# A third layer as 7 block products for 8, with its weights streamed for each token block

## The chip, the cores and the metric

The kernel runs on one NeuronCore of one Trainium2 chip. The metric is the device time of one execution, in microseconds (us). The kernel before takes 916.54 us (median of 3 runs, 916.5 to 916.63).

## The reference

Attention over 4 batches, 8 heads, 576 positions of 64 (window of 32 positions in half of the heads, the same dilated by 4 in the others) gives `x` of 2304 tokens by 512. Two feed-forward networks follow it, all in float32:

```python
x    = attention(q, k, v)                       # [2304, 512]
gate = 1.0 / (1.0 + np.exp(-(x @ w_gate)))      # 512 -> 1536
y    = (gate * (x @ w_val)) @ w_out             # 1536 -> 512
h    = y @ w_in                                 # 512 -> 2048, the "third layer"
g    = np.maximum(h, 0.0) + alpha * np.minimum(h, 0.0)
out  = g @ w_out2                               # 2048 -> 512
```

The weights come as float64 and are decoded on the chip.

## The kernel before

Every float32 product is made of three passes of float16 matmuls: each operand is scaled by a power of two and split into a high half `hi` and the rest `lo`, and hi·hi, hi·lo and lo·hi are added in PSUM (`passes`, L476). The high half is a ScalarE (ACT) activation, the low half a VectorE (DVE) instruction that reads the source and the high half (`split_act`, L168 to L170); weights use `split_weight` (L198), two ACT passes and a subtraction on POOL (L166).

The work falls into four stages. The first follows a list written out by hand (`FIRST`): attention of batch 0 and its gate and value products, until about 180 us. Then a loop over batches 1 to 3 does twelve steps of gate and value products (`gv_mm`, L588, 288 columns) and four of the second layer (`o1_mm`, L630, 72 matmuls each). Attention of the next batch is put between them by two tables (`before`, `after`): softmax on DVE and POOL, a 32x32 transpose (L404), its halves (`p_hi` on ACT L408, `p_lo` on POOL L166) and the product with the values on TensorE (PE) (L435). Between all of this `prepare` runs `steps`, the decoding and splitting of the last two layers' weights, as a budget of columns allows: of `w_in` the split is done by `in2_split` and stored to `wi_dram`; of `w_out2` seven block sums are built (`out2_sums`, DVE, L767 to L770), split (L777 ACT, L782 DVE) and stored to `w2_dram`. During batch 3 four tiles `w_i` (1 MB each, all of `w_in` in halves) are loaded and stay.

The last stage begins at 556.9 us and is what the change rewrites. The 2304 tokens go in five blocks, four of 512 and one of 256. For each block the third layer has 16 column tiles (`in2_mm`, L836 to L849: 12 matmuls each, 512 tokens wide, into one of four PSUM banks). Each tile is evicted by `in2_evac`: ACT takes relu(-h) (L881), DVE adds alpha times it to h (the slope, L882). Tiles k and k + 8 are a pair: `g_sums` makes four block sums of it on POOL (L893 to L896, 256 wide), and seven parts are split, highs on ACT (`g_high`, L905), lows on DVE (`g_low`, L908). The fourth layer already runs as 7 block products for 8: `out2_mm` (L925 to L946) is an item (product i, pair k) of 6 matmuls 256 wide, 56 items a block; its weights come through a ring of four 1 MB slots (`w2_fetch`, L916 to L923, 35 fetches). The items of a block are put between the tiles of the next block, 3 or 4 behind each. `out2_done` (L948 to L967) evicts a product and writes the result. The next block's activations come by `y_load` (L826) and `y_split` (L828). PE runs in program order, and so does each other engine; a tile's bank comes free when its slope on DVE is done.

## Time and profile before

| what | before |
|---|---|
| median of 3 runs | 916.54 us (916.5 to 916.63) |
| the profiled execution | 915.95 us, span 914.2 us |
| mean granted TensorE clock | 0.966 |
| busy: PE, DVE, ACT, POOL | 868.0, 620.9, 447.9, 285.8 us |
| last stage, 556.9 to 910.4 us | 353.5 us: PE busy 352.56, DVE 233.17, ACT 169.86, POOL 122.17 |
| bytes moved by DMA | 131.08 MB |

The page gives the busy time of each engine over the span of one profiled execution; the span is 1.75 us shorter than that execution's own time. The granted clock is TensorE's as a share of 2.4 GHz. A timeline row has the start, the length, the engine, the line and the operation, and in brackets the idle time before it with the work that ended it. Matmuls overlap, so the price of one in a stream is the distance between the starts of two rows divided by the count, not a row's length.

### The profile page before, as it was taken

How to read it: one execution, taken by the hardware profiler on the slowest of the kernel's cores; microseconds unless marked ns; L12 is line 12 of the kernel's file. 1: busy time of each engine (PE TensorE's matmuls, PEld its weight loads, DVE VectorE, ACT ScalarE, POOL GpSimd, SP SyncE). 2: the span in 40 equal slices, each digit the busy share in tenths (PEclk: the TensorE clock that was granted, in tenths of full speed). 3: DMA queues.
4: the chain of work that ended last, by engine and by line, in shares of the span. 5: the costliest groups of instructions: out<-in, count | busy, mean ns of one | idle time of the engine just before them, and what ended most of it. 6: DMA issues, size and time to landing. Idle time of an engine off the chain costs nothing.

```text
span 914.2 us, 18416 instructions
## 1 busy us (share of the span) xinstructions
PE 868.0 (95%) x7636; PEld 645.8 (71%) x7636; DVE 620.9 (68%) x1004; ACT 447.9 (49%) x821; POOL 285.8 (31%) x311
## 2 busy tenths in 40 slices
PE   7878888899999799999999999999999999999998
PEld 5566666687777577877888775456666666667887
DVE  5999999724767455667775662996666676667452
ACT  4776565445344466434434554674444444444441
...
GB/s 322 270 229 119 158 108 161 39 59 178 49 50 174 136 145 217 25 1 165 240 162 196 210 258 273 79 46 105 57 164 137 104 116 127 104 105 123 144 161 219
DMA packets 114179, 131.08 MB, mean 143 GB/s; under 512 B 33200, under 2 KB 100912, under 8 KB 109104
## 3 DMA queue, kind: packets, MB, share of 16 engines
...
## 4 chain that ended last, share of the span: by engine, by line
PE 74%; DVE 16%; ACT 3%; DMA 3%; issue 2%; POOL 1%; SPq 0%; DVEq 0%; POOLq 0%; ACTq 0%
PE banks L588 22%; PE banks L846 20%; PE banks L939 18%; PE banks L630 10%; DVE plain L181 4%; PE banks L435 3%; DVE plain L185 3%; DVE plain L177 2%; DVE gf L606 1%; DMA words<-w_gate 1%; PE banks L321 1%; DVE rs L379 1%; DMA second<-kt 1%; DVE vh L280 1%; POOL s L166 1%
## 5 line engine op out<-in xcount | busy, mean ns | idle before, releaser
L588 PE MATMUL banks<-xh,w_gv 128*128 128x288 f16 x2304 | 297.7, 291 | 0.1
L588 PEld LDWEIGHTS <-w_gv 128*128 128x128 f16 x2304 | 226.4, 99 | 61.0
L846 PE MATMUL banks<-yh,w_i 128*128 128x512 f16 (+1 forms) x960 | 197.6, 358 | 0.9 <-DVE yh L170 0.9
L846 PEld LDWEIGHTS <-w_i 128*128 128x128 f16 x960 | 93.8, 98 | 83.6 <-issue 1.5
L630 PE MATMUL banks<-gt,w_o 128*128 128x288 f16 x1152 | 151.0, 295 | 0.1
L630 PEld LDWEIGHTS <-w_o 128*128 128x128 f16 x1152 | 114.6, 101 | 32.5 <-DVE w_o L170 0.6
L881 ACT ACTIVATE neg<-banks 128x512 f32<-128x512 f32 (+1 forms) x80 | 44.0, 550 | 140.7 <-PE banks L846 140.7
L939 PE MATMUL banks<-w,g_g 128*128 128x256 f16 x600 | 76.8, 273 | 0.0
L606 DVE SCALAR_TENSOR_TENSOR gf<-banks,sg 128x576 f32<-128x576 f32 x48 | 36.1, 752 | 57.7 <-PE banks L588 53.0
L939 PE MATMUL banks<-w,g_o 128*128 128x256 f16 x570 | 73.7, 273 | 0.0
L192 ACT ACTIVATE junk<-plain 128x1024 bf16<-128x1024 f32 (+1 forms) x36 | 36.3, 1007 | 75.9 <-DVE plain L196 42.2
L882 DVE SCALAR_TENSOR_TENSOR f<-neg,sc,banks 128x512 f32<-128x512 f32 (+1 forms) x40 | 27.7, 692 | 60.6 <-ACT neg L881 60.6
L939 PEld LDWEIGHTS <-g_g 128*128 128x128 f16 x600 | 58.7, 98 | 10.9
L181 DVE SCALAR_TENSOR_TENSOR plain<-words,plain 128x512 uint32<-128x512 uint32 x68 | 64.1, 963 | 1.2
L939 PEld LDWEIGHTS <-g_o 128*128 128x128 f16 x570 | 55.8, 98 | 10.5
L882 DVE SCALAR_TENSOR_TENSOR temps_a<-neg,sc,banks 128x512 f32<-128x512 f32 (+1 forms) x40 | 27.7, 693 | 52.2 <-ACT neg L881 52.2
L166 POOL TENSOR_TENSOR gt<-gf,gt 128x576 f16<-128x576 f32 x24 | 37.4, 1558 | 79.8 <-ACT gt L613 79.8
L185 DVE SCALAR_TENSOR_TENSOR plain<-words,plain 128x512 uint32<-128x512 uint32 x68 | 58.9, 886 | 1.2
L893 POOL TENSOR_TENSOR temps_a<-f,f 128x256 f32<-128x256 f32 (+1 forms) x20 | 16.4, 818 | 133.2 <-DVE f L882 133.2
L601 ACT ACTIVATE sg<-banks,sc 128x576 f32<-128x576 f32 x48 | 35.2, 734 | 39.3 <-PE banks L588 34.7
L613 ACT ACTIVATE gt<-gf 128x576 f16<-128x576 f32 x48 | 32.4, 676 | 42.0 <-DVE gf L606 42.0
L162 POOL TENSOR_SCALAR sc<-sc 128x1 f32<-128x1 f32 (+1 forms) x35 | 11.9, 340 | 129.2 <-DVE sc L158 119.6
...
## 6 DMA issues: line engine op xcount, KB each, us to landing
w<-w_dram SPq DMA_DIRECT2D x35, 1024.0 KB, 5.0
...
```

The costliest lines, as they stand in the source:

```text
L166: engine.tensor_tensor(out=lo, in0=src, in1=hi, op=ALU.subtract)
L181: nc.vector.scalar_tensor_tensor(out=d, in0=hi, scalar=0xC0000000, in1=d, op0=ALU.bitwise_and, op1=ALU.bitwise_or)
L185: nc.vector.scalar_tensor_tensor(out=d, in0=lo, scalar=29, in1=d, op0=ALU.logical_shift_right, op1=ALU.bitwise_or)
L192: nc.scalar.activation(junk[:, :src.shape[1]], src, AF.Square, accum_out=dst)
L588: nc.tensor.matmul(ps[:, h, :], lhsT=a, rhs=x_[:, H2 * h:H2 * h + H2], start=(kk == 0 and i == 0), stop=(kk == KD - 1 and i == 2),)
L601: nc.scalar.activation(halves(sg), ps, AF.Sigmoid, scale=sgx[b][:, m:m + 1])
L606: nc.vector.scalar_tensor_tensor(out=halves(gf), in0=ps, scalar=2.0 ** -15, in1=halves(sg), op0=ALU.mult, op1=ALU.mult)
L630: nc.tensor.matmul(ps[:, h, :], lhsT=a, rhs=x_[:, H2 * h:H2 * h + H2], start=(m == 0 and z == 0), stop=(m == M1 - 1 and z == 2),)
L846: nc.tensor.matmul(ps[:, :n], lhsT=a, rhs=x_, start=(kk == 0 and i == 0), stop=(kk == KD - 1 and i == 2))
L881: nc.scalar.activation(t[:, :n], ps[:, :n], AF.Relu, scale=-1.0)
L882: nc.vector.scalar_tensor_tensor(out=gf[:, :n], in0=t[:, :n], scalar=slope[:, m:m + 1], in1=ps[:, :n], op0=ALU.mult, op1=ALU.add)
L939: nc.tensor.matmul(ps[:, H4 * t:H4 * t + H4], lhsT=a, rhs=x_, start=(first and k == 0 and t == 0 and z == 0), stop=(k == U - 1 and z == 2) ...
```

## The change

The third layer becomes 7 block products for 8 too. In four blocks of 512 tokens, tokens, inputs and columns are halved into quarters, and seven products of sums of quarters (P1 to P7, the Winograd form of Strassen's scheme) give the four quarters of h. A block has four units (`unit`), each of 7 products of 12 matmuls 256 wide; behind each product come two items of the fourth layer (`spare`). Products that belong together are added in PSUM; where they aren't, ACT copies a bank to SBUF (`copy`) and DVE adds the next product to the copy (`plus`). A relu is 512 wide still, a slope two instructions 256 wide, a split of a part 512 wide for what were two of 256. The block of 256 tokens comes first, as plain products (`unit_short`, two tiles at once: an x product on three banks in turn, a y product always on the same bank).

The weights of the third layer are now seven blocks for four and don't all stay: `wi_dram` holds 8 pieces of 896 KB, two of which make a unit's, and for every block all 8 are fetched, into four slots (block 0: also the four slots of the fourth layer's ring, which is not needed yet). A unit gives its two slots back at its end, and only then are the next two pieces and the fourth layer's weights fetched, in SP's queue. Building them takes 4 DVE additions for each u (`in2_sums`), the highs go to ACT and the lows to DVE, so that POOL's subtraction of 1024 columns is gone; in return `out2_sums` moves from DVE to POOL, as do sums of quarters of y (`y_sums`). `prepare` has a larger budget.

```diff
     H4 = DM // 2
     TB = 512
     scale = 0.125
-    blocks = [(t, min(TB, NT - t)) for t in range(0, NT, TB)]
+    T0 = NT % TB
+    blocks = [(0, T0)] + [(t, TB) for t in range(T0, NT, TB)]
     NJ = len(blocks)
+    DIRECT = 0
...
+    wi_dram = dp.tile([U, P, 2, 7, 2 * P], F16, name="wi_dram")
...
+    def in2_sums(u):
+        a21, a11, a12, a22 = (plain["i", u][:, 2 * i:2 * i + 2] for i in range(4))
+        t = plain["is", u] = yp.tile([P, 4, 2, P], F32, tag="y", name="is")
+        add = nc.vector.tensor_tensor
+        add(out=t[:, 0], in0=a21, in1=a22, op=ALU.add)
+        add(out=t[:, 1], in0=t[:, 0], in1=a11, op=ALU.subtract)
+        add(out=t[:, 2], in0=a11, in1=a21, op=ALU.subtract)
+        add(out=t[:, 3], in0=a12, in1=t[:, 1], op=ALU.subtract)
...
-    def in2_split(u):
-        w = plain["ih", u] = yp.tile([P, 2, 4, 256], F16, tag="y", name="halves")
-        t = flat(plain.pop(("i", u))).rearrange("p (k f) -> p k f", k=4)
-        split_weight(w[:, 0], w[:, 1], t, s_i[:, 2 * u:2 * u + 1])
...
+    def in2_high(u):
+        plain["ih", u] = [yp.tile([P, 2, n, 2 * P], F16, tag="y", name="halves") for n in (3, 4)]
+        for w, src in in2_parts(u):
+            nc.scalar.activation(w[:, 0].rearrange("p n f -> p (n f)"), src, AF.Copy, scale=s_i[:, u:u + 1])
+
+    def in2_low(u, i):
+        w, src = in2_parts(u)[i]
+        nc.vector.scalar_tensor_tensor(
+            out=w[:, 1].rearrange("p n f -> p (n f)"), in0=src, scalar=s_i[:, u:u + 1],
+            in1=w[:, 0].rearrange("p n f -> p (n f)"), op0=ALU.mult, op1=ALU.subtract,
+        )
...
+    def in2_fetch(u, ring=ring_i):
+        if not ring_i and not w_i:
+            ring_i.extend(w2p.tile([P, 2, 7, 2 * P], F16, name=f"w_i{n}", tag=f"w_i{n}") for n in range(4))
+        t = ring.popleft()
+        homes.append((ring, t))
+        if ring is not ring_i:
+            t = t.rearrange("p z u f -> p (z u f)")[:, :14 * 2 * P].rearrange("p (z i f) -> p z i f", z=2, i=7)
+        w_i.append(t)
+        nc.sync.dma_start(out=t, in_=wi_dram[u])
+
+    def in2_release():
+        for _ in range(2):
+            w_i.popleft()
+            ring, t = homes.popleft()
+            ring.append(t)
...
-        add = nc.vector.tensor_tensor
+        add = nc.gpsimd.tensor_tensor
...
+    def y_sums(j, d):
...
+        s = y[j, d, "sums"] = yp.tile([P, 4, TB // 2], F32, tag="y", name="ys")
+        add = nc.gpsimd.tensor_tensor
+        if j == DIRECT:
+            add(out=s[:, 0, :n], in0=t[:, 1, :n], in1=t[:, 0, :n], op=ALU.subtract)
+            return
+        b11, b12, b21, b22 = (t[:, i, n // 2 * h:n // 2 * h + n // 2] for i in range(2) for h in range(2))
+        add(out=s[:, 0], in0=b12, in1=b11, op=ALU.subtract)
+        add(out=s[:, 1], in0=b22, in1=s[:, 0], op=ALU.subtract)
+        add(out=s[:, 2], in0=b22, in1=b12, op=ALU.subtract)
+        add(out=s[:, 3], in0=b21, in1=s[:, 1], op=ALU.subtract)
...
+    PART_A = {1: 0, 2: 1, 4: 2, 5: 3, 6: 4, 7: 5, 3: 6}
+    PART_B = {1: 0, 2: 1, 3: 2, 5: 3, 6: 4, 7: 5, 4: 6}
+    in2_banks = {}
+    in2_order = []
+
+    def in2_bank(x_):
+
+        turn["h"] = (turn["h"] + (x_ != "y")) % 3
+        in2_banks[x_] = banks[:, in2_order[3 if x_ == "y" else turn["h"]], :]
...
+        total_ = len(terms) * 6
+        for v in range(2):
+            o = ps[:, n * v:n * v + n]
+            q = 0
+            for a, b in terms:
+                for d in range(2):
+                    c = slice(P * d, P * d + P)
+                    for h, l in passes((w[v][:, 0, a, c], w[v][:, 1, a, c]), (yh[j][0][:, d, b, :n], yh[j][1][:, d, b, :n])):
+                        q += 1
+                        nc.tensor.matmul(
+                            o, lhsT=h, rhs=l, start=(new and v == 0 and q == 1), stop=(q == total_),
+                            skip_group_check=True,
+                        )
         return ps
 
...
+    def unit_short(j, k, spare):
+
+        w = [w_i[0], w_i[1]]
+        u = 2 * k
+        ps = in2_mm(j, "x", [(0, 0), (1, 1)], True, w)
+        spare(3)
+        sums_high()
+        sums_low(4)
+        prelu(j, u, "a11 0", ps)
+        spare(4)
+        ps = in2_mm(j, "y", [(3, 0), (2, 2)], True, w)
+        spare(4)
+        prelu(j, U + u, "a12", ps)
+        a11, a21, a12, a22 = quarters(j, k)
+        parts = [g_high(j, i, k, x_) for i, x_ in ((1, a11), (4, a22), (2, a12))]
+        for t in parts:
+            g_low(*t)
+        spare(3)
+        s = g_sums(j, k)
+        late_.extend((j, i, k, x_) for i, x_ in s)
+
+
+
+    left = [[] for _ in range(7)]
+    begun_units = set()
+
+    def unit_begin(j, k, w):
+        begun_units.add((j, k))
+        copy("c1", in2_mm(j, "x1", [(PART_A[1], PART_B[1])], True, w))
+
+    def unit(j, k, spare, following=None):
+        w = [w_i[0], w_i[1]]
+        u = 2 * k
+        a11, a21, a12, a22 = quarters(j, k)
+        f11 = temps[f"a11 {k % 2}"]
+        t, h = {}, {}
+        if (j, k) not in begun_units:
+            unit_begin(j, k, w)
+        in2_banks["x"] = in2_banks.pop("x1")
+
+        def mm(i, x_, new=False):
+            return in2_mm(j, x_, [(PART_A[i], PART_B[i])], new, w)
+
+        def rest(i):
+            for f in left[i]:
+                f()
+            left[i] = []
+
+        def later(i, f):
+            left[i].append(f)
+
+        def high(i, x_):
+            h[i] = g_high(j, i, k, x_)
+
+        ps = mm(2, "y", True)
+        rest(0)
+        nc.vector.tensor_tensor(out=f11, in0=ps, in1=temps["c1"], op=ALU.add)
+        spare()
+        copy("c2", mm(6, "x"))
+        t["a11"] = relu(j, f11)
+        rest(1)
+        slopes(j, u, f"a11 {k % 2}", f11, t["a11"])
+        spare()
+        ps_z = mm(7, "z", True)
+        rest(2)
+        high(1, a11)
+        g_low(*h[1])
+        spare()
+        copy("c4", mm(5, "x"))
+        rest(3)
+        plus("a22", "c4", ps_z)
+        spare()
+        if following:
+            unit_begin(*following, [w_i[2], w_i[3]])
+        t["a22"] = relu(j, temps["a22"])
+        rest(4)
+        slopes(j, U + u, "a22", temps["a22"], t["a22"])
+        spare()
+        ps = mm(3, "x")
+        t["a21"] = relu(j, ps)
+        high(4, a22)
+        slopes(j, u, "a21", ps, t["a21"])
+        g_low(*h[4])
+        (_, s1), (_, a21), (_, s2), (_, s4) = g_sums(j, k, last=False)
+        spare()
+        plus("a12", "c2", mm(4, "z"))
+        spare()
+
+        later(0, lambda: prelu(j, U + u, "a12", temps["a12"]))
+        later(1, lambda: (high(2, a12), high(5, s1), g_low(*h[2]), g_low(*h[5]), g_sums(j, k, first=False)))
+        later(2, lambda: (high(7, a21), g_low(*h[7])))
+        later(3, lambda: (high(6, s2), g_low(*h[6])))
+        later(4, lambda: (high(3, s4), g_low(*h[3])))
...
-            if k == U - 1 and ring and fetched:
+            if k == U - 1 and j == NJ - 1:
+                w2_fetch_all()
+
+        def w2_fetch_all():
+            while ring and fetched:
...
-                prepare(2)
+                prepare(3)
...
+        for j in range(NJ):
+            for k in range(U // 2):
+                if j == 0:
+                    if k == 1:
+                        for i in range(3, NJ):
+                            y_sum(i)
+                        for i in range(3, NJ):
+                            y_power(i)
+                    assert not steps, len(steps)
+                if k == 0:
+                    total_scale(j)
+                if 0 < j < NJ - 1:
+                    if k == 0:
+                        y_load(j + 1)
+                    if k in (1, 2):
+                        y_sums(j + 1, k - 1)
+                if j == DIRECT:
+                    unit_short(j, k, spare)
+                else:
+                    n = (j, k + 1) if k + 1 < U // 2 else (j + 1, 0)
+                    unit(j, k, spare, n if n[0] not in (DIRECT, NJ) else None)
+                if 0 < j < NJ - 1 and k in (1, 2):
+                    y_high(j + 1, k - 1)
+                    y_low(j + 1, k - 1)
+                in2_release()
+                while coming and ring_i:
+                    in2_fetch(coming.popleft())
+                w2_fetch_all()
+            if j in (DIRECT, NJ - 1):
+                flush()
+                sums_high()
+                sums_low(4)
```

The order of the instructions on three queues shows what moves. First POOL, in batch 1's second layer, where attention of batch 2 is under way: L386 and `s<-pt,s` are attention (softmax scaling and `p_lo`), `halves` is the weights' subtraction of `split_weight`, `sc` are single scales. Before:

```order
L386 TENSOR_TENSOR s<-s,rs 128x1152
L162 TENSOR_SCALAR sc<-sc 128x2
L166 TENSOR_TENSOR halves<-plain,halves 128x1024
L639 TENSOR_SCALAR sc<-sc 128x1
L162 TENSOR_SCALAR sc<-sc 128x2
L166 TENSOR_TENSOR halves<-plain,halves 128x1024
L639 TENSOR_SCALAR sc<-sc 128x1
L166 TENSOR_TENSOR s<-pt,s 128x1152
```

and with the change (its own line numbers: L388 is L386, L168 is L166, L641 is L639):

```order
L388 TENSOR_TENSOR s<-s,rs 128x1152
L641 TENSOR_SCALAR sc<-sc 128x1
L164 TENSOR_SCALAR sc<-sc 128x1
L641 TENSOR_SCALAR sc<-sc 128x1
L168 TENSOR_TENSOR s<-pt,s 128x1152
```

Two subtractions of 1024 columns that stood between the two attention rows are no longer on POOL.

Second ACT, in the last stage. Before, around tiles k and k + 8 of block 0, L881 is a relu and L905 a high half of 256 columns:

```order
L881 ACTIVATE neg<-banks 128x512
L905 ACTIVATE g_o<-temps_a,sc 128x256 x3
L881 ACTIVATE neg<-banks 128x512
L905 ACTIVATE g_o<-temps_c,sc 128x256
L905 ACTIVATE g_o<-temps_a,sc 128x256
L905 ACTIVATE g_o<-temps_c,sc 128x256 x2
L881 ACTIVATE neg<-banks 128x512
L905 ACTIVATE g_o<-f_6646,sc 128x256
```

With the change, at the end of block 0 and the start of block 1 (L1023 are high halves, L1000 the copies c1 and c2 of block 1's first unit, L983 a relu):

```order
L983 ACTIVATE neg<-banks 128x512 x2
L1023 ACTIVATE g_g<-temp_y,sc 128x256 x3
L1023 ACTIVATE g_s<-temp_w,sc 128x256
L1023 ACTIVATE g_s<-temp_y,sc 128x256
L1023 ACTIVATE g_s<-temp_w,sc 128x256
L1023 ACTIVATE g_s<-temp_y,sc 128x256
L1000 ACTIVATE temp<-banks 128x512 x2
L983 ACTIVATE neg<-temp_y 128x512
L1023 ACTIVATE g_y<-temp_y,sc 128x512
```

Four late high halves of block 0's last unit now stand ahead of the copy that block 1's third product needs.

Third SP's queue of DMA issues, at the start of the last stage. Before (`w` is the fourth layer's ring, `out` the result):

```order
L826 DMA y<-y_dram 128x2x512 x2
L923 DMA w_6725<-w_dram 128x4096 x2
L964 DMA out<-ob 128x2x256
L923 DMA w_6726<-w_dram 128x4096 x2
L964 DMA out<-ob 128x2x256
L923 DMA w_6725<-w_dram 128x4096
L964 DMA out<-ob 128x2x256
L923 DMA w_6725<-w_dram 128x4096
```

With the change, from the first unit of block 1 on (`w_i` are pieces of the third layer's weights, L757):

```order
L871 DMA y<-y_dram 128x2x512 x2
L757 DMA w_i_5832<-wi_dram 128x3584
L757 DMA w_i_5833<-wi_dram 128x3584
L1167 DMA w_6336<-w_dram 128x4096
L1209 DMA out<-yh 128x256
L757 DMA w_i_5834<-wi_dram 128x3584
L757 DMA w_i_5835<-wi_dram 128x3584
L1167 DMA w_6336<-w_dram 128x4096
L1167 DMA w_6337<-w_dram 128x4096
```

Two pieces of `w_i` are now fetched at the end of each unit, in one queue with the ring's weights.

## Rows read from the trace of the kernel before

**Rows 1.** The profile page's first section, one row: busy time, share, instructions.

```profile
PE 868.0 (95%) x7636; PEld 645.8 (71%) x7636; DVE 620.9 (68%) x1004; ACT 447.9 (49%) x821; POOL 285.8 (31%) x311
```

**Rows 2.** Three windows: block 0, blocks 1 to 3, block 4; busy us by engine, PEclk.

```profile
556.90:602.40 45.50, 44.56 (x220) 20.26 (x218) 36.84 (x70) 30.56 (x63) 20.18 (x27) 1.00 0.39 146
602.40:834.20 231.80, 231.80 (x1574) 153.76 (x1572) 157.95 (x247) 111.84 (x239) 84.13 (x101) 1.00 0.32 111
834.20:910.40 76.20, 76.20 (x699) 68.06 (x696) 38.38 (x92) 27.46 (x81) 17.86 (x36) 1.00 0.49 175
```

**Rows 3.** Groups of TensorE by shape, 557 to 912 us: busy us, mean ns, idle before.

```profile
L846 PE MATMUL banks<-yh,w_i 128*128 128x512 f16 x768 | 174.0, 379 | 0.9 <-DVE yh L170 0.9
```

**Rows 4.** TensorE's timeline, 825 to 850 us: start, length, work, idle before in brackets.

```profile
829.05 2.75 PE L846 MATMUL banks<-yh,w_i 128*128 128x512 f16 x12
831.64 1.47 PE L939 MATMUL banks<-w,g_o 128*128 128x256 f16 x12
...
834.26 1.47 PE L846 MATMUL banks<-yh,w_i 128*128 128x256 f16 x12
835.57 0.82 PE L939 MATMUL banks<-w,g_y 128*128 128x256 f16 x6
```

**Rows 5.** TensorE's timeline, 595 to 625 us: its one gap in the last stage.

```profile
601.42 1.24 PE L846 MATMUL banks<-yh,w_i 128*128 128x512 f16 x5 [0.94 <-DVE yh L170]
```

**Rows 6.** TensorE's timeline, 280 to 450 us: around attention's products.

```profile
291.94 4.57 PE L630 MATMUL banks<-gt,w_o 128*128 128x288 f16 x36
...
303.83 2.69 PE L435 MATMUL banks<-s,vh 64*128 64x64 f16 x53 [6.96 <-POOL s L166]
306.45 5.97 PE L630 MATMUL banks<-gt,w_o 128*128 128x288 f16 x36
...
427.69 1.84 PE L435 MATMUL banks<-s,vh 64*128 64x64 f16 x53 [2.11 <-POOL s L166]
```

**Rows 7.** POOL's timeline, 280 to 330 us.

```profile
298.82 2.12 POOL L166 TENSOR_TENSOR halves<-plain,halves 128x1024 f16<-128x1024 f32 x1 [2.75 <-ACT halves L203]
...
301.42 2.36 POOL L166 TENSOR_TENSOR s<-pt,s 128x1152 f16<-128x1152 f32 x1
```

**Rows 8.** POOL's timeline, 560 to 605 us: first block sum alone, then in DVE's company.

```profile
563.85 0.72 POOL L893 TENSOR_TENSOR temps_a<-f,f 128x256 f32<-128x256 f32 x1 [35.55 <-DVE f L882]
...
575.34 0.90 POOL L893 TENSOR_TENSOR temps_a<-f,f 128x256 f32<-128x256 f32 x1 [2.15 <-DVE f L882]
```

**Rows 9.** VectorE's timeline, 560 to 605 us: four lows of block 0.

```profile
575.17 0.48 DVE L908 SCALAR_TENSOR_TENSOR g_o<-temps_c,sc,g_o 128x256 f16<-128x256 f32 x1
575.57 0.95 DVE L908 SCALAR_TENSOR_TENSOR g_o<-temps_a,sc,g_o 128x256 f16<-128x256 f32 x1
576.45 1.81 DVE L908 SCALAR_TENSOR_TENSOR g_o<-temps_c,sc,g_o 128x256 f16<-128x256 f32 x2
```

**Rows 10.** Groups of VectorE by shape, 180 to 914 us.

```profile
L882 DVE SCALAR_TENSOR_TENSOR f<-neg,sc,banks 128x512 f32<-128x512 f32 x32 | 23.8, 745 | 49.7 <-ACT neg L881 49.7
...
L177 DVE TENSOR_SCALAR plain<-words 128x512 uint32<-128x512 uint32 x32 | 15.4, 480 | 16.8 <-POOL halves L166 11.0 <-DMA plain_dram<-plain 3.0 <-ACT junk L192 2.7
...
L782 DVE SCALAR_TENSOR_TENSOR halves<-plain,sc,halves 128x512 f16<-128x512 f32 x12 | 10.8, 915 | 1.0 <-ACT halves L777 1.0
L170 DVE SCALAR_TENSOR_TENSOR yh<-y,sc,yh 128x1024 f16<-128x1024 f32 x8 | 10.3, 1285 | 5.0 <-ACT yh L169 5.0
```

**Rows 11.** Groups of ScalarE by shape, 180 to 914 us.

```profile
L881 ACT ACTIVATE neg<-banks 128x512 f32<-128x512 f32 x64 | 37.9, 592 | 111.2 <-PE banks L846 111.2
L905 ACT ACTIVATE g_o<-temps_a,sc 128x256 f16<-128x256 f32 x44 | 21.1, 498 | 4.5 <-DVE temps_a L882 3.8 <-POOL temps_a L896 0.4 <-POOL temps_a L895 0.4
```

**Rows 12.** DMA issues of the whole run: KB each, median us from issue to landing.

```profile
w<-w_dram SPq DMA_DIRECT2D x35, 1024.0 KB, 5.0
```

**Rows 13.** DMA issues from 560 to 590 us, when several fetches stand together.

```profile
w<-w_dram SPq DMA_DIRECT2D x3, 1024.0 KB, 12.8
```

**Rows 14.** VectorE's timeline, 890 to 915 us: the last eviction.

```profile
910.45 0.48 DVE L959 SCALAR_TENSOR_TENSOR ob<-banks,sc,temps_c 128x256 f32<-128x256 f32 x1 [2.13 <-PE banks L939]
```

More of the change, by code (lines that the diff above doesn't have):

```diff
@@ new lines, in in2_store @@
+    def in2_store(u):
+        for t, r in zip(plain.pop(("ih", u)), (slice(0, 3), slice(3, 7))):
+            nc.sync.dma_start(out=wi_dram[u][:, :, r], in_=t)
+    ring_i = deque()
+    w_i = deque()
+    homes = deque()
+    def in2_fetch(u, ring=ring_i):
[7 more added lines that the diff above has]
+        nc.sync.dma_start(out=t, in_=wi_dram[u])
@@ L836, in in2_mm @@
[L836 to L848 removed]
+        for d in range(2):
+            t = y[j, d] = yp.tile([P, 2, TB], F32, tag="y", name="y")
+            nc.sync.dma_start(out=t[:, :, :n], in_=y_dram[:, d::2, t0:t0 + n])
@@ new lines, in relu, with slopes @@
+    def relu(j, src):
+        n = blocks[j][1] if j == DIRECT else TB // 2
+        t = tp.tile([P, TB], F32, tag="sg", name="neg")
+        nc.scalar.activation(t[:, :2 * n], src[:, :2 * n], AF.Relu, scale=-1.0)
+        return t
+    def slopes(j, u, x_, src, t):
+        n = blocks[j][1] if j == DIRECT else TB // 2
+        for v in range(2):
+            c = slice(n * v, n * v + n)
+            nc.vector.scalar_tensor_tensor(
+                out=temps[x_][:, c], in0=t[:, c], scalar=slope[:, u + v:u + v + 1], in1=src[:, c], op0=ALU.mult,
+                op1=ALU.add,
+            )
@@ new lines, in prelu, with copy, plus, quarters @@
+    def prelu(j, u, x_, src):
+        slopes(j, u, x_, src, relu(j, src))
+    def copy(x_, ps):
+        nc.scalar.activation(temps[x_], ps, AF.Copy)
+    def plus(x_, c, ps):
+        nc.vector.tensor_tensor(out=temps[x_], in0=ps, in1=temps[c], op=ALU.add)
+    def quarters(j, k):
+        if j == DIRECT:
+            n = blocks[j][1] // 2
+            return [
+                temps[x_][:, :4 * n].rearrange("p (v h t) -> p v h t", v=2, h=2)[:, :, h, :]
+                for x_ in ("a11 0", "a12") for h in range(2)
+            ]
+        return [temps[x_].rearrange("p (v t) -> p v t", v=2) for x_ in (f"a11 {k % 2}", "a21", "a12", "a22")]
@@ L882, in in2_evac, with g_place, g_high, g_low @@
+    def g_place(j, i, k):
+        n = blocks[j][1] // 2
+        h = places2.popleft()
+        g2[j, i, k] = [h, 2]
+        return h[:, :, :2 * n].rearrange("p z (v t) -> p z v t", v=2)
+    def g_high(j, i, k, x_):
+        h = g_place(j, i, k)
+        nc.scalar.activation(h[:, 0], x_, AF.Copy, scale=s_al)
+        return h, x_
+    def g_low(h, x_):
         nc.vector.scalar_tensor_tensor(
-            out=gf[:, :n], in0=t[:, :n], scalar=slope[:, m:m + 1], in1=ps[:, :n], op0=ALU.mult, op1=ALU.add
+            out=h[:, 1], in0=x_, scalar=s_al, in1=h[:, 0], op0=ALU.mult, op1=ALU.subtract
@@ L1151, in attention_moe_kernel @@
                 do(after, m)
-                prepare(2 - (0 if late else ATTENTION.get(m, 0)), sums=False)
+                prepare(3 - (0 if late else ATTENTION.get(m, 0)), sums=False)
                 if late and m in (5, 7, 9, 11):
```

272 lines of the change are left out of this document (137 added, 135 removed).

## The prediction

> **What bounds the kernel now.** I read the page's busy times first, then windows over the last stage, then TensorE's timeline for the price of one matmul, then its gaps, and last the prices on the other engines. PE is busy 868.0 of 914.2 us [rows 1], and in the last stage 352.56 of 353.5 [rows 2], always at full clock (the 1.00 in those rows, so 2.4 GHz). Busy rows of overlapping matmuls count more than their share (one reads 379 ns there [rows 3]), so the price is taken from starts: twelve 512 wide begin at 829.05 and the next work at 831.64, 2.59 us or 215.8 ns each; twelve 256 wide begin at 834.26 and the next at 835.57, 1.31 us or 109.2 ns each [rows 4]. The stage holds 768 of the wide kind [rows 3] and 192 + 1512 of the narrow (the small block's third layer; 56 items of 6 matmuls in four blocks, of 3 in one): 768 x 0.2158 + 1704 x 0.1092 = 351.8 us. That is the stage but for 1.7 us, of which one wait is 0.94 [rows 5]. So PE's columns are the stage, and what shortens them counts as long as nothing else becomes the bound. Elsewhere two gaps stand out, 6.96 and 2.11 us ahead of attention's products of batches 2 and 3 [rows 6].
>
> **Columns.** The third layer now issues 192 + 16 units x 84 = 1536 matmuls 256 wide in place of 768 wide and 192 narrow ones. The stage's 3048 at 0.1092 come to 332.8: against the stage's 353.5 that is **-20.7**. The narrow ones each load weights for half the columns; the rows show no cost for that, since the fourth layer does the same now and the 109.2 ns are taken from it. The Trainium skill, TensorE: Matmul & The Clock Gate, section Back-to-back issue gap, gives about 131 ns for a matmul 512 wide and 81 ns for one 128 wide in a sustained stream of weight loads and matmuls. By it the wide matmuls that go would be worth 100.6 us and the 1344 that come between 109 and 176 (an estimate from those two figures), a loss of 8 to 75. The trace does not agree: both widths stand here in one sustained stream at 215.8 and 109.2 ns, so it gets no chance.
>
> **Attention.** In batch 1 the first gap ends with POOL's `s<-pt,s` at 301.42 + 2.36, and ahead of that POOL subtracts 1024 columns for 2.12, from 298.82 on [rows 7]. With the change two such subtractions are gone from between POOL's two attention instructions. That alone is 4.2 us, the lower bound of the gain. DVE, whose transpose starts the chain, waited 11.0 us in all for POOL's subtractions to free a buffer before it could decode [rows 10] and no longer does, so more can go: both gaps, 9.1, and the slow stretch behind the first, 36 matmuls in 5.97 us against 4.57 [rows 6], 1.4. Against it DVE and ACT get the lows and highs of seven blocks for four, queued among the same attention steps; I put 1.5 on that. Taken: **-9.0**, between -4 and -11.8. The four additions in `in2_sums`, the larger budget and `out2_sums` on POOL lie beside gate and value products and cost nothing as long as these keep PE fed; if the cover failed, it would show as gaps like those two.
>
> **Block 0.** A short unit needs 48 x 0.1092 = 5.24 us of PE and has nothing to fill with. Its chain on the others is longer, from the end of y's slopes to the same point one unit later: four POOL sums in DVE's company, 0.72 alone and up to 0.90 beside DVE [rows 8], 3.4 together; the third low that the fourth sum waits for, 0.5 [rows 9]; the last late high, 0.5, and the relu queued behind it, 0.59 [rows 11]; x's and y's slopes, each twice 256 wide at 0.48, the price of a low of that width [rows 9], 1.9. Together 6.9. The y product always takes the same bank, so PE waits for that chain: 1.7 for each of the third and fourth unit, 3.3. At the change to block 1 it waits twice more. P2 takes the y bank: 6.9 less y's own product and P1 (3.9) is 3.0. P6 adds onto P1's bank, which c1 must have copied, and c1 stands in ACT's queue behind the four late highs: 3.4 + 0.5 + 0.5 + 0.59 after those slopes, while P2 and two small items fill 2.0: 3.0 again. A pause like this was followed by slower matmuls in batch 1, 1.4 as above. Together **+10.7**. Lower bound 3, the transition's second wait alone; upper 18, if all three units and the first slopes wait and lows go at 0.95, as one does beside POOL [rows 9].
>
> **Blocks 1 to 4.** DVE has per unit three additions 512 wide at 0.745, the price of a slope of that width, seven lows 512 wide between 0.745 and 0.915 (the row of the weights' lows of that size) [rows 10], eight slopes at 0.48 and 0.6 of evictions: 11.9 to 13.1. The units that also split y add lows of 256, 512 and 1024 columns, 0.48 + 0.745 + 1.285 [rows 9, 10] = 2.5. PE has 168 x 0.1092 = 18.35 in blocks 2 to 4, so DVE hides. In block 1 the items are half as large, and PE has 126 x 0.1092 = 13.76: two units of four come to 14.4 to 15.6 on DVE, and POOL's sums delay some lows. I take **+4**, between 0 (queues even out) and 12. ACT's three copies and four relus at 0.59 and seven highs at no more than twice 0.498 [rows 11] come to 11 us a unit and hide.
>
> **Weights.** Each unit's end issues two pieces of 896 KB and one or two of 1 MB. They have until P1 of the unit after next: four products and four pairs of items, then a product more, 9 x 1.31 = 11.8 us in blocks 2 to 4. A fetch lands in 5.0 when alone [rows 12] and in 12.8 when four stand with four loads of y, 6 MB [rows 13]; 2.9 to 3.9 MB by that rate take 6 to 9. Hidden; the cover is that one unit of PE.
>
> **Tail.** The last eviction and its store are now of a block of 512: against 0.48 now [rows 14] the eviction takes the 0.745 of its width, and the store of twice the bytes, which no row prices, I put at 0.6 more, between 0 and 1.2: **+0.9**.
>
> **Sum.** -20.7 - 9.0 + 10.7 + 4 + 0.9 = -14.1 from the profiled execution's 915.95 gives 901.85; the median of the runs lies 0.6 above that execution, so 902.4, and I say **902**.
>
> **Rivals.**
> - **The gaps in attention stay.** Only the two subtractions move; p_lo still waits for a transpose that DVE does late, behind more work of its own. For it: DVE has more instructions there now; against: POOL's wait ended last. 902.4 + 9 = 911. 0.15.
> - **Block 0 hides.** ACT and DVE catch up while x's three banks let PE run ahead: 902.4 - 10.7 = 891.5. 0.11.
> - **DVE becomes the bound in block 1** and in the y units of blocks 2 and 3. For it: a low beside POOL takes 0.95 for 0.48 [rows 9], so the 6 to 7 us of POOL sums per unit could cost DVE 2.5 in each. Block 1 then loses 14 in place of 4, blocks 2 and 3 another 2.6: 915. 0.10.
> - **DVE and POOL shut each other out.** Only one of them runs where a low meets a sum: 12.0 + 5.8 per unit, 5.4 more where y is split. Block 1 loses 27 in place of 4 and blocks 2 and 3 about 17: 942. Against it: a sum of 0.72 takes 0.90 in company [rows 8], not 0.72 and a whole low, and four lows beside POOL's four sums run from 575.17 to 578.26 [rows 9], 3.1 us where 1.9 + 2.9 would be 4.8. 0.03. The Trainium skill, SBUF — State Buffer, section Who interferes with whom, states this: a DVE instruction with two SBUF inputs contends with a GpSimd one that reads SBUF, and the loser blocks for the whole instruction. The rows agree that both grow longer and do not show that one fully stops.
> - **Slower: the pieces arrive late.** They are asked for only when a unit ends. If landing takes the 12.8 of four fetches standing together [rows 13], each of twelve units in blocks 2 to 4 waits 1.0, and three in block 1, whose time is about 8.5, wait 4.3: +25, 927. It decides once landing passes 11.8. Against: half as many bytes stand together. 0.07.
> - That the change doesn't do what it says is not open: the third layer's instructions stand in the program as described, 84 for 96 narrow ones' worth.
>
> **How the numbers follow.** The forecast has 0.54, with its own bounds at 894 to 909. The range is 888 to 916: it takes in the cases at 891.5, 911 and 915 with some room below for blocks 0 and 1 both at their lower bounds, and leaves out 927 and 942. A measurement of this kernel tells 0.2% from no change, 1.8 us. Faster by more (under 914.7) are the forecast, the first two rivals and half of the third, less the tails: 0.85. Within it 0.05. Slower (over 918.4): the last two, 0.10.
>
> **What would show it.** PE's windows after: in blocks 2 to 4 no idle time, and twelve matmuls in 1.31. In block 0 and at block 1's first unit PE idle ended by DVE slopes and by ACT's copy, about 9 us. In batch 1's second layer POOL's `s` right behind p_hi, and the gap ahead of the product with the values under 2 us. It would be wrong if PE waits for `w_i` by a DMA, if DVE is busy over nine tenths in blocks 2 to 4, or if twelve narrow matmuls take more than 1.31 when their weights change with every one.

## The result, and the profile after

The changed kernel takes 922.89 us (median of 4 runs, 921.14 to 923.12) against 916.59 (4 runs, 916.5 to 918.26): ratio 1.0060, 95% interval 1.0043 to 1.0078. It is slower by 0.6%, where 902 was forecast. The profile shown is of an execution of 922.71 us with a span of 920.8.

The page, which answers to [rows 1]:

```profile
PE 846.8 (92%) x8196; PEld 698.1 (76%) x8196; DVE 685.9 (74%) x1039; ACT 451.5 (49%) x739; POOL 317.3 (34%) x273
...
PEclk9799899899999999999999997998999999999999
```

PE is busy 21 us less than before, and the span is 6.6 us longer. So PE waits. TensorE's timeline has the waits (idle time in brackets); the last stage begins with the first of these rows:

```profile
559.99 7.89 PE L948 MATMUL banks<-yh,w_i 128*128 128x256 f16 x48 [15.34 <-ACT y L646]
...
582.40 2.79 PE L948 MATMUL banks<-yh,w 128*128 128x256 f16 x24 [0.89 <-DVE temp_y L991]
585.03 1.47 PE L948 MATMUL banks<-yh,w_i 128*128 128x256 f16 x12
588.70 2.48 PE L948 MATMUL banks<-yh,w_i 128*128 128x256 f16 x12 [2.19 <-DVE temp_y L991]
...
593.30 1.47 PE L948 MATMUL banks<-yh,w_i 128*128 128x256 f16 x12 [0.84 <-ACT temp L1000]
...
597.22 1.47 PE L948 MATMUL banks<-yh,w_i 128*128 128x256 f16 x12
598.53 0.82 PE L1184 MATMUL banks<-w,g_g 128*128 128x256 f16 x6
...
635.90 2.72 PE L948 MATMUL banks<-yh,w_i 128*128 128x256 f16 x12 [5.95 <-ACT temp_y L1000]
638.41 1.48 PE L1184 MATMUL banks<-w,g_s 128*128 128x256 f16 x6
...
654.87 1.47 PE L948 MATMUL banks<-yh,w_i 128*128 128x256 f16 x12 [2.96 <-ACT temp_y L1000]
```

The second layer ended at 559.99 - 15.34 = 544.65; before it ended at 556.90 [rows 2]. Then PE stands still for 15.34 us. Block 1's first product starts at 585.03, its third (P6) at 593.30, where two products (P1 and P2) and two items of block 0, half as long, would have needed 3.3 us. Undisturbed, twelve matmuls still take 1.31 us (597.22 to 598.53). In block 1 PE waits 5.95 and 2.96 more, and is slow behind the first of them (12 matmuls in 638.41 - 635.90 = 2.51 us for 1.31). Windows from the second layer's end, with the start gap, block 0, the transition with block 1, and the rest (columns as in [rows 2]; the number ahead of the DMA share is the granted clock):

```profile
544.65:559.99 15.34, 0.00 (x1) 0.00 (x1) 7.34 (x9) 7.89 (x14) 10.35 (x13) 0.61 0.85 222
559.99:585.03 25.04, 24.14 (x206) 20.11 (x206) 17.58 (x39) 14.51 (x30) 9.78 (x13) 0.90 0.69 247
585.03:656.34 71.31, 58.44 (x496) 50.01 (x494) 57.22 (x85) 38.17 (x66) 30.47 (x26) 0.93 0.53 202
656.34:917.70 261.36, 258.75 (x2364) 230.96 (x2362) 193.55 (x270) 119.92 (x197) 95.70 (x68) 1.00 0.54 207
```

The account: the second layer ends 12.2 us earlier. The gap takes 15.3. The last stage, from its first matmul to the end of its last (559.99 to 916.8), takes 356.8 us for 353.5 before [rows 2]: its columns are 332.8, so 24.0 are lost: block 0 4.1 (25.0 for 20.96 of columns, 2.5 of them slow clock behind the gap: the first 48 matmuls take 7.7 us for 5.24, and the granted clock of this window is 0.90), transition 5.0 (waits of 2.19 and 0.84, and 1.8 of slow clock behind the first), block 1 12.0 (0.93 + 5.95 + 2.96 and 2.1 of slow clock), later waits 1.7, the rest 1.2. With 0.1 at the tail, -12.2 + 15.3 + 3.3 + 0.1 = +6.5.

What held PE for 15.3 us stands in three queues. ScalarE:

```profile
540.31 0.72 ACT L822 ACTIVATE halves<-plain,sc 128x512 f16<-128x512 f32 x1 [5.00 <-DMA w_dram<-halves]
...
548.43 0.51 ACT L911 ACTIVATE yh<-ys,sc 128x256 f16<-128x256 f32 x1 [6.79 <-POOL ys L901]
...
558.16 1.15 ACT L911 ACTIVATE yh<-ys,sc 128x1024 f16<-128x1024 f32 x1 [1.85 <-POOL ys L907]
559.21 0.72 ACT L646 ACTIVATE y<-banks,sc 128x576 f32<-128x576 f32 x1
```

POOL:

```profile
547.67 1.53 POOL L901 TENSOR_TENSOR ys<-y 128x256 f32<-128x256 f32 x2 [17.69 <-DMA w_dram<-halves]
```

PE needs a bank that ACT frees with the eviction L646 at 559.21. Ahead of it on ACT stand block 1's highs of y (L911), which wait for POOL's sums. Ahead of those sums on POOL stand block 0's (L901), which wait for a buffer until a store of w_out2's halves to `w_dram` lands at 547.5. The stores are slow: issues from 500 to 545 us (KB each, us to landing):

```profile
w_dram<-halves SPq DMA_DIRECT2D x34, 128.0 KB, 5.5
w<-wi_dram SPq DMA_DIRECT2D x4, 896.0 KB, 6.3
```

Two theories followed: the order on ACT and the buffers make the gap (theory 1), or the bytes of the early fetches `w<-wi_dram` do, by making the stores late (theory 2).

### The profile page after: what moved, and what is told of

It reads as the page before. It is cut to its first block, busy times and chain, and to the rows that moved or that the text cites. A ratio compares the mean times of both kernels' runs of the same rounds, so it can differ in the third digit from the quotient of the medians.

```text
span 920.8 us, 19481 instructions
## 1 busy us (share of the span) xinstructions
PE 846.8 (92%) x8196; PEld 698.1 (76%) x8196; DVE 685.9 (74%) x1039; ACT 451.5 (49%) x739; POOL 317.3 (34%) x273
## 4 chain that ended last, share of the span: by engine, by line
PE 47%; DVE 33%; DMA 7%; ACT 6%; issue 4%; SPq 2%; POOL 1%; ACTq 0%; POOLq 0%; DVEq 0%
PE banks L590 18%; PE banks L1184 10%; PE banks L632 8%; PE banks L948 7%; DVE temp_y L991 5%; DVE plain L183 4%; DVE yh L915 3%; DVE plain L187 3%; DMA w_dram<-halves 3%; DVE plain L179 3%; PE banks L437 2%; DVE g_o L1027 2%; DMA w_i<-wi_dram 1%; DVE g_g L1027 1%; ACT g_o L1023 1%
## 5 line engine op out<-in xcount | busy, mean ns | idle before, releaser
L948 PE MATMUL banks<-yh,w_i 128*128 128x256 f16 x1440 | 181.0, 277 | 30.0 <-ACT y L646 15.3
L948 PEld LDWEIGHTS <-w_i 128*128 128x128 f16 x1440 | 143.0, 99 | 50.8 <-issue 29.2
L632 PE MATMUL banks<-gt,w_o 128*128 128x288 f16 x1152 | 147.4, 290 | 0.9 <-POOL gt L168 0.8
L991 DVE SCALAR_TENSOR_TENSOR temp_y<-neg,sc,temp_y 128x256 f32<-128x256 f32 x96 | 77.7, 849 | 8.2 <-ACT neg L983 8.1
L1037 POOL TENSOR_TENSOR temp_w<-temp_y 128x512 f32<-128x512 f32 (+1 forms) x20 | 31.1, 1554 | 148.1 <-DVE temp_y L991 148.1
L164 POOL TENSOR_SCALAR sc<-sc 128x1 f32<-128x1 f32 x35 | 13.5, 385 | 166.9 <-DVE sc L160 166.8
L1184 PE MATMUL banks<-w,g_g 128*128 128x256 f16 x564 | 69.4, 273 | 0.0
L1184 PEld LDWEIGHTS <-g_g 128*128 128x128 f16 x564 | 55.2, 98 | 6.4
L168 POOL TENSOR_TENSOR gt<-gf,gt 128x576 f16<-128x576 f32 x24 | 36.4, 1516 | 63.9 <-ACT gt L615 63.9
L983 ACT ACTIVATE neg<-temp_y 128x512 f32<-128x512 f32 x48 | 30.1, 628 | 56.8 <-DVE temp_y L1111 28.5
L179 DVE TENSOR_SCALAR plain<-words 128x512 uint32<-128x512 uint32 x68 | 39.8, 606 | 12.3 <-DMA plain_dram<-plain 6.8
```

What stands on the lines that cost most here:

```text
L168: engine.tensor_tensor(out=lo, in0=src, in1=hi, op=ALU.subtract)
L179: nc.vector.tensor_scalar(out=d, in0=hi, scalar1=3, scalar2=0x3FFFFFFF, op0=ALU.logical_shift_left, op1=ALU.bitwise_and)
L632: nc.tensor.matmul(ps[:, h, :], lhsT=a, rhs=x_[:, H2 * h:H2 * h + H2], start=(m == 0 and z == 0), stop=(m == M1 - 1 and z == 2),)
L948: nc.tensor.matmul(o, lhsT=h, rhs=l, start=(new and v == 0 and q == 1), stop=(q == total_), skip_group_check=True,)
L991: nc.vector.scalar_tensor_tensor(out=temps[x_][:, c], in0=t[:, c], scalar=slope[:, u + v:u + v + 1], in1=src[:, c], op0=ALU.mult, op1=ALU.add,
L1184: nc.tensor.matmul(ps[:, H4 * t:H4 * t + H4], lhsT=a, rhs=x_, start=(first and k == 0 and t == 0 and z == 0), stop=(k == U - 1 and z == 2) ...
```

## Experiments: the gap ahead of the last stage

**e1_y1_late, e2_ys_apart, e3_both.** In e1 block 1's split of y moves from the second layer into block 0:

```diff
-                    if late and 1 <= d < 3 and m == 2:
+                    if late and d == 1 and m == 2:
...
-                    if late and 1 <= d < 3 and m in (4, 8):
+                    if late and d == 1 and m in (4, 8):
...
-                if 0 < j < NJ - 1 and k in (1, 2):
+                if j < NJ - 1 and k in (1, 2):
                     y_high(j + 1, k - 1)
```

> Block 1's split of y (block sums on POOL, highs on ACT, lows on DVE) is moved from the second layer's column 2 of batch 3 into units 1 and 2 of block 0. Theory 1 (order and slots): those highs stand in ACT's queue ahead of the last two evictions of the second layer, and cost 8 of the 15.3 us gap; the other 7 come from block 0's own sums, which get their buffer only when a store lands at 547.5. So the gap becomes about 7, the whole about 915 with 1 us given back in block 0. Theory 2 (DMA load): the eight pieces of w_i fetched in the second layer keep the queues full and every store late, so another wait takes the place: gap 12 or more, 920 or more.

In e2 block 0's sums have their own place; e3 has both edits:

```diff
+            if d == 0:
+                temps["ys"] = w2p.tile([P, 2, TB], F32, name="ys0", tag="temp_w")
+            s = y[j, d, "sums"] = temps["ys"][:, d:d + 1, :]
```

> Block 0's block sums of y get a place of their own (the tile temp_w, unused until then) instead of a slot of the ring that the stores of w_out2 hold. Theory 1: block 0's highs no longer wait for the store at 547.5 and ACT is through with them at about 542; but block 1's sums still take two slots of the ring, and its highs still stand ahead of the evictions, so the gap only falls to 10 to 14: 918 to 922. Theory 2: no change, 922 to 923, gap 15.

> Both edits: block 1's split in block 0, block 0's sums in a place of their own. Theory 1: the second layer's last evictions follow each other at once, the gap falls below 2 us, and with it the slow clock behind it (2.5 us): 904 to 908. Theory 2: the gap stays at 10 or more, 917 or more.

Measured: e1 921.87 (one run, gap 6.88), e2 925.5 (one run, gap 14.82), e3 922.12 (4 runs, ratio 1.0046, 1.0028 to 1.0064, gap 3.57). Only e1's gap fell as theory 1 said. e2's hardly moved, which theory 2 had expected, and e3's lies between what the two expected. No time fell. e3's timeline shows why:

```profile
549.37 7.06 PE L951 MATMUL banks<-yh,w_i 128*128 128x256 f16 x48 [3.57 <-ACT y L646]
...
578.74 5.30 PE L951 MATMUL banks<-yh,w 128*128 128x256 f16 x24 [4.74 <-DVE temp_y L994]
```

PE starts 10.6 us earlier, but the split of y in block 0 lengthens the chain there, and 4.74 and other waits take the gain back: P6 of block 1 starts at 591.80, only 1.5 us earlier. The order alone was not it.

**e4_w_late.** Only the four later ones of the eight early fetches move:

```diff
-                    if late and d == 0 and m in (3, 5, 7, 9):
+                    if late and d == 3 and m in (3, 5, 7, 9):
                         in2_fetch(4 + m // 2 - 1, ring)
```

> The last four of the eight early pieces of w_i (3.6 MB) are asked for in the second layer's column 3 instead of column 0; nothing else moves. Theory 2: the stores of w_out2 land earlier, the slot for block 0's sums is free some 5 us or more before 547.5, and the gap falls to 5 to 9: 912 to 917. Theory 1: the bytes matter little, the gap shrinks by 3 at most: 919 to 923.

Measured: 912.69 (one run), 10.2 less than the change. The gap, and the stores from 500 to 545 us:

```profile
549.98 8.14 PE L948 MATMUL banks<-yh,w_i 128*128 128x256 f16 x48 [5.99 <-ACT y L646]
```

```profile
w_dram<-halves SPq DMA_DIRECT2D x44, 128.0 KB, 2.7
```

The stores land in 2.7 us for 5.5, and the gap falls from 15.34 to 5.99. Theory 2 holds for most of the gap.

**e13_bytes_back, e14_issues_only.** Do bytes count, or the issues in SP's queue? Both are e4 with the early fetches again (n = 7: all of each piece; n = 1: a seventh), which the later ones overwrite:

```diff
+                    if late and d == 0 and m in (3, 5, 7, 9):
+                        t = ring[m // 2 - 1].rearrange("p z u f -> p (z u f)")[:, :14 * 2 * P]
+                        t = t.rearrange("p (z i f) -> p z i f", z=2, i=7)
+                        nc.sync.dma_start(out=t[:, :, :n], in_=wi_dram[4 + m // 2 - 1][:, :, :n])
```

> e4_w_late (912.7) with the four pieces of w_i (3.6 MB) fetched in column 0 as well, into the same places and used by nobody before the second fetch in column 3 has overwritten them. If the load of those bytes on the DMA queues is what made the stores of w_out2 late, the 15 us gap is back though every consumer waits for the same later fetch: stores land in about 5.5 us from 500 to 545 us, 920 to 924. If the gain of e4 came from elsewhere (what waits for those places), 912 to 914.

> The same with a seventh of each piece (128 KB) in column 0: the four issues in SP's queue stay where they were, the bytes go. If bytes count, 912 to 914, stores land in about 2.7 us; if it is the issues that stand in SP's queue among the stores, 918 or more.

Measured: 924.61 with the bytes back (4 runs, ratio 1.0069, 1.0052 to 1.0086), 916.17 with the issues and a seventh (10 runs, 0.9985, 0.9973 to 0.9996). Gap and stores of the first:

```profile
562.46 7.40 PE L948 MATMUL banks<-yh,w_i 128*128 128x256 f16 x48 [15.66 <-ACT y L646]
```

```profile
w_dram<-halves SPq DMA_DIRECT2D x34, 128.0 KB, 5.2
```

and of the second:

```profile
553.77 7.85 PE L948 MATMUL banks<-yh,w_i 128*128 128x256 f16 x48 [9.03 <-ACT y L646]
```

```profile
w_dram<-halves SPq DMA_DIRECT2D x39, 128.0 KB, 3.8
```

e14's time and landing lie between what its two cases expected. In e13 all of the cost is back though every consumer waits for the same later fetch. Of the 9.7 us between 5.99 and 15.66, 3.0 come with the issues and a seventh of the bytes, 6.6 with the rest: it is mostly the bytes. Whether those 3.0 belong to the issues or to their 0.5 MB stays open.

**e8_y1_d3, e9_sums_d3.** With the load gone the order is worth something: in e8 block 1's highs and lows go behind the eviction of column 2 (`d in (1, 3)` for `1 <= d < 3`, `d // 2` for `d - 1`), in e9 its sums too.

> Built on e4_w_late. Highs and lows of block 1's y are moved from the second layer's column 2 to column 3, behind the eviction of column 2, which frees two banks; the block sums on POOL stay. If what is left of the gap at the start of the last stage (5.99 us) is this order on ACT, it falls below 1.5, the chain of block 0 begins 3 to 5 us earlier: 907 to 910. If the gap is still a matter of late loads, 912 to 913.

> Built on e8_y1_d3 (909.7). Block 1's sums on POOL follow its highs into column 3, behind the scale of column 2's eviction, which stood behind them on POOL. The last 3.1 us of the gap should go and the clock stay up: PE runs from the second layer into the third without a wait, 905 to 908. If something else holds the eviction (the store of y behind SP's other issues, say), 909 to 910.5.

Measured: 909.71 (one run), then 906.46 (4 runs from 905.26 to 912.6, ratio 0.9901, 0.9876 to 0.9926). With such a spread e8's 3.0 us would show little by themselves, but the gap fell by as much. In e8 3.11 us of it were left, where less than 1.5 was expected, since the scale of the eviction stood behind block 1's sums on POOL; in e9 PE goes from one layer to the next without a wait:

```profile
539.79 5.80 PE L632 MATMUL banks<-gt,w_o 128*128 128x288 f16 x46
545.43 5.40 PE L948 MATMUL banks<-yh,w_i 128*128 128x256 f16 x48
```

## Experiments: attention, block 0, block 1

**e5_low_on_pool.** The lows of w_in's products are POOL's again, with ACT scaling the source first; the DVE instruction of `in2_low` goes:

```diff
+            nc.scalar.activation(src, src, AF.Copy, scale=s_i[:, u:u + 1])
...
+        rest(nc.gpsimd, w[:, 1].rearrange("p n f -> p (n f)"), src, w[:, 0].rearrange("p n f -> p (n f)"))
```

> Built on e4_w_late (912.7). The lows of w_in's seven block products go back to POOL as subtractions (of 768 and 1024 columns each, with ACT scaling the source first), as the kernel before did for its one. If POOL's subtractions ahead of attention's p_lo made the gaps of 6.96 and 2.11 us, they come back at batches 2 and 3, 7 us or more together with the slower clock: 919 to 924. If the gaps went for another reason (the larger budget, the other order of the steps), they stay away: 912 to 915.

Measured: 925.69 (one run), 13.0 more than e4. The edit also gives ACT one more pass, but the waits that come back end with POOL's work. The gaps ahead of attention's products come back, 9.4 us together:

```profile
298.96 2.69 PE L437 MATMUL banks<-s,vh 64*128 64x64 f16 x53 [3.53 <-POOL s L168]
...
427.36 2.69 PE L437 MATMUL banks<-s,vh 64*128 64x64 f16 x53 [5.83 <-POOL s L168]
```

In the change those waits were 0.52 and none:

```profile
296.56 1.58 PE L437 MATMUL banks<-s,vh 64*128 64x64 f16 x53 [0.52 <-POOL s L168]
...
415.83 1.63 PE L437 MATMUL banks<-s,vh 64*128 64x64 f16 x54
```

**e6_banks.** Block 0's products take four banks in turn.

```diff
+        if len(in2_short) < U:
+            in2_short.append(x_)
+            in2_banks[x_] = banks[:, in2_order[len(in2_short) % 4], :]
+            return
```

> Built on e4_w_late. Block 0's eight products take the four banks in turn, so that y's product no longer waits for one fixed bank. If that bank makes PE wait, the waits ahead of block 0's last y product (0.89) and of P2 of block 1 (2.19) go, and 2 to 3 us with them: 909.5 to 911. If the chain over POOL, ACT and DVE sets the time whatever the bank, PE only waits later, at P6 for the copy c1: 912 to 913.

Measured: 913.92 (one run), no gain. The waits in block 0 went, and the transition's two grew from 2.19 and 1.09 to:

```profile
577.95 1.48 PE L953 MATMUL banks<-yh,w_i 128*128 128x256 f16 x12 [2.66 <-DVE temp_y L996]
...
583.33 2.72 PE L953 MATMUL banks<-yh,w_i 128*128 128x256 f16 x12 [3.24 <-ACT temp L1005]
```

The chain over POOL, ACT and DVE sets the time; the bank only says where PE waits for it.

**e7_no_sums.** POOL fills the sums' tiles with a constant (`nc.gpsimd.memset` for each `add` of `g_sums`), so this kernel leaves out the block sums of g. In the change VectorE's groups from 585 us on were (mean ns behind the busy time; slopes from SBUF, slopes from PSUM, two lows of y):

```profile
L991 DVE SCALAR_TENSOR_TENSOR temp_y<-neg,sc,temp_y 128x256 f32<-128x256 f32 x96 | 77.7, 849 | 8.2 <-ACT neg L983 8.1
...
L991 DVE SCALAR_TENSOR_TENSOR temp_y<-neg,sc,banks 128x256 f32<-128x256 f32 x36 | 15.5, 475 | 0.6 <-ACT neg L983 0.6
...
L915 DVE SCALAR_TENSOR_TENSOR yh<-ys,sc,yh 128x1024 f16<-128x1024 f32 x6 | 13.7, 2284 | 0.0
...
L915 DVE SCALAR_TENSOR_TENSOR yh<-y,sc,yh 128x512 f16<-128x512 f32 x6 | 10.5, 1755 | 0.0
```

> Built on e4_w_late. POOL's four block sums of each unit (and of block 0) are left out: POOL fills the four tiles with a constant instead, which reads nothing, so the seven parts of g are not those of the reference. If DVE's instructions with two SBUF sources and POOL's sums shut each other out, the slopes from SBUF fall from 849 ns to below 500, the y lows of 1024 columns from 2141 to about 1300 but where y's own sums on POOL still meet them, and the waits of block 1 (0.94, 5.96 and 2.85 us) fall below 3 together: 901 to 905. If DVE is bound by its own instructions, the durations hardly move and the waits stay: 910 to 913.

Measured: 897.97 (one run), 14.7 less than e4, with these groups:

```profile
L991 DVE SCALAR_TENSOR_TENSOR temp_y<-neg,sc,temp_y 128x256 f32<-128x256 f32 x94 | 45.9, 529 | 6.4 <-ACT neg L983 6.4
...
L915 DVE SCALAR_TENSOR_TENSOR yh<-ys,sc,yh 128x1024 f16<-128x1024 f32 x6 | 7.7, 1278 | 0.0
...
L915 DVE SCALAR_TENSOR_TENSOR yh<-y,sc,yh 128x512 f16<-128x512 f32 x6 | 4.5, 746 | 0.0
```

The same instructions on the same data sizes take 529 for 849, 1278 for 2284 and 746 for 1755 ns, and block 1's waits on ACT and DVE fall from 9.84 us to 1.65 (with 1.50 more on a late piece of w_i). But a fill is also shorter than a sum (524 ns for 1322 to 1735 in e4), so e7 shortens POOL's own part of the chain as well, and its 14.7 is not the price of the meetings alone. One meeting in the change shows what happens. VectorE's low of 1024 columns, and POOL's sum:

```profile
645.32 2.28 DVE L915 SCALAR_TENSOR_TENSOR yh<-ys,sc,yh 128x1024 f16<-128x1024 f32 x1
```

```profile
644.81 1.71 POOL L1039 TENSOR_TENSOR temp_w<-temp_w,temp_y 128x512 f32<-128x512 f32 x1
```

The sum ends at 646.52; the low, begun at 645.32, ends at 647.60, 1.08 us behind it. Without sums it takes 1.28, so in the 1.20 us beside the sum it got on by 0.20 at most: it all but stood still until the sum was done. A pair of slopes from SBUF, first in the change beside a sum, then in e7 beside a fill:

```profile
651.70 1.88 DVE L991 SCALAR_TENSOR_TENSOR temp_y<-neg,sc,temp_y 128x256 f32<-128x256 f32 x2
...
651.26 1.64 POOL L1041 TENSOR_TENSOR temp_y<-temp_y,temp_w 128x512 f32<-128x512 f32 x1 [4.74 <-DVE g_o L1027]
```

```profile
598.05 0.87 DVE L991 SCALAR_TENSOR_TENSOR temp_y<-neg,sc,temp_y 128x256 f32<-128x256 f32 x2
...
598.19 0.52 POOL L1037 MEMSET temp_w<- 128x512 f32 x1
```

The fill, which reads nothing, cost the pair nothing: 0.87 is also what a pair takes in the change while POOL is idle (at 647.53). The Trainium skill, SBUF — State Buffer, section Who interferes with whom, says that a DVE instruction with two SBUF inputs contends with a GpSimd one that reads SBUF, not with one that only writes it, and that the loser blocks; these rows agree.

**e10_inplace, e11_ysums_dve.** e9 with two of a unit's additions written back to PSUM (relu and slopes then read them there), so that four of six slopes have only one source in SBUF:

```diff
-        nc.vector.tensor_tensor(out=f11, in0=ps, in1=temps["c1"], op=ALU.add)
+        nc.vector.tensor_tensor(out=ps, in0=ps, in1=temps["c1"], op=ALU.add)
...
-        plus("a12", "c2", mm(4, "z"))
+        ps_z = mm(4, "z")
+        nc.vector.tensor_tensor(out=ps_z, in0=ps_z, in1=temps["c2"], op=ALU.add)
```

> Built on e9_sums_d3. Two of the three additions of a unit are written back to their PSUM bank, so that four of the six slopes that read two SBUF sources now read one and PSUM. If the meeting of two-source DVE instructions with POOL's sums is what block 1 pays for, those slopes take about 475 ns for 850 and block 1's waits (0.9, 6.0 and 3.0) fall to 3 to 6 together: 3 to 6 us under e9, 901 to 904. If only DVE's own length counts, or POOL now meets the next low instead, 1 us or less under e9.

Measured: 901.39 (6 runs from 899.02 to 906.33, ratio 0.9841, 0.9816 to 0.9867), 5.1 under e9; block 1's waits are 0.21, 3.25 and 2.22. POOL's sums are all still there, so this is the meetings' price without the objection to e7, and only in part: some meetings move to lows of g (29 of them take 816 ns on average for 748 in e9). The slopes:

```profile
L991 DVE SCALAR_TENSOR_TENSOR temp_y<-neg,sc,banks 128x256 f32<-128x256 f32 x96 | 41.7, 475 | 6.7 <-ACT neg L983 6.6
...
L991 DVE SCALAR_TENSOR_TENSOR temp_y<-neg,sc,temp_y 128x256 f32<-128x256 f32 x32 | 14.0, 478 | 1.9 <-ACT neg L983 1.9
```

From PSUM (475 ns) or from SBUF with hardly any meeting left (478) a slope takes the same: it is the company that costs, not the second source by itself. e11 then moves y's block sums to DVE.

> Built on e10_inplace. The block sums of y for blocks 2 to 4 move from POOL to DVE (eight additions of 256 columns a block). If shutting out costs more than DVE's own time, 1 to 3 us under e10; if block 1 is bound by DVE's own instructions by now, 1 to 3 us over it.

Measured: 903.97 (4 runs, 0.9864, 0.9851 to 0.9877). Its interval overlaps e10's: no gain, a loss not settled. y's lows of 1024 columns stayed at 2282 ns, so it is the sums of g, not those of y, that they meet.

**e12_y_later.** e10 with y's highs and lows behind the next unit's fifth product:

```diff
-                    y_high(j + 1, k - 1)
-                    y_low(j + 1, k - 1)
+                    left[3].append(lambda a=(j + 1, k - 1): (y_high(*a), y_low(*a)))
```

> Built on e10_inplace (901.4). The highs and lows of y for blocks 2 to 4 move from a unit's end, where POOL has just begun three block sums, to behind the fifth product of the next unit, when POOL's last sum is done; the number of instructions stays. If the lows are long because they meet POOL's sums (2284 and 1756 ns for 1024 and 512 columns, against 1278 and 746 without sums in e7), they fall near the latter and block 1's waits with them: 1 to 3 us under e10, 898 to 900.5. If their place doesn't matter, 901 to 902.

Measured: 909.88 (6 runs, 0.9918, 0.9904 to 0.9932), 8.5 over e10. The lows did get shorter:

```profile
L915 DVE SCALAR_TENSOR_TENSOR yh<-ys,sc,yh 128x1024 f16<-128x1024 f32 x6 | 8.8, 1466 | 1.0 <-ACT yh L911 1.0
...
L915 DVE SCALAR_TENSOR_TENSOR yh<-y,sc,yh 128x512 f16<-128x512 f32 x6 | 4.5, 744 | 0.0
```

but the second half of y is now ready only after the next block's first product, which stands in the same unit, has begun, and PE waits for it at each of three blocks, 7.8 us together. The longest wait:

```profile
633.26 0.27 PE L948 MATMUL banks<-yh,w_i 128*128 128x256 f16 x1 [3.05 <-ACT yh L911]
```

This missed both cases that were expected. The best version is e10, 1.6% faster than the kernel before.

## Why the prediction was wrong

- **The step that failed: the sum has no term for what the change adds ahead of the last stage.** "Weights" ends in "Hidden", but it priced only the fetches for blocks 1 to 4, which do arrive in time. The eight early fetches, 7.3 MB for 4.2 before, in a stretch where w_out2's stores fill the queues, were priced at nothing, without a reason. So were the splits of y that the change puts ahead of the evictions on ACT. Together they cost 15.3 us of standing still and 2.5 of slow clock. e4 and e13 show the bytes, e8 and e9 the order (6.2 more). Without those 17.8 the change would stand at about 905; e9, which is that, measured 906.5.
- **Block 1, +4: mis-sized, 12.0 measured,** the upper bound given. Slopes were priced at 0.48 and the lows of a unit that splits y at 2.5, and that is what they take undisturbed (475 and 478 ns in e10; 0.48 + 0.75 + 1.28 = 2.5 in e7). Beside POOL's sums the six of eight slopes with two SBUF sources took 0.85 on average and y's lows 4.7 (0.69 + 1.76 + 2.28).
- **DVE and POOL shut each other out, 0.03: that was the mechanism of this loss.** The argument against it misread its rows, as shown below. The price (942) was far too high, since it let every low meet a sum, and the sign doesn't come from here. How much of the 12 us is the meetings is shown in part: e10 takes 5.1 us off. How the rest divides between the lows and the length of POOL's own sums stays open.
- **Columns, -20.7: right.** Twelve narrow matmuls take 1.31 us after as before, wherever PE doesn't wait. (19.0 of the term is columns, 351.8 to 332.8; 1.7 is the waits of the stage before.)
- **Attention, -9.0: right in cause, too small.** The second layer ends 12.2 us earlier, just past the bound of -11.8, a bound for which the working gives only 9.1 + 1.4 = 10.5. e5 shows that POOL's subtractions make such gaps; that they are all of the 12.2 isn't shown.
- **Block 0 and transition, +10.7: too large, within its bounds.** 9.1 measured, but 2.5 of it is the slow clock behind the gap, counted above, so 6.6 are their own; that 9.1 stands near 10.7 is luck. And the bank that was named as the reason was only the place (e6).
- **The slower rival** had late weights, but at another place: pieces for P1 in blocks 1 to 4, where the change has no wait on a fetch.
- **Tail, +0.9:** 0.1.

The rows against the shut-out were 3.1 us for four lows beside four sums. But the fourth sum began when the last low (it ended at 578.26 [rows 9]) was nearly through:

```profile
578.05 0.79 POOL L896 TENSOR_TENSOR temps_a<-f,temps_a 128x256 f32<-128x256 f32 x1
```

And the low begun at 575.57 ended at 576.52 [rows 9], only 0.28 us behind the end of the sum at 575.34 + 0.90 = 576.24 [rows 8], though one takes 0.48 alone: most of it came after the sum. The waiting was there to be read before the change.

None of the three signs of being wrong came: PE never waits for `w_i` in the last stage, DVE is 74% busy from 656.34 on (193.55 of 261.36), and twelve matmuls take 1.31. All three looked into the stage that was rewritten, and the larger loss stood ahead of it.
